# Block sums of the second layer's weights in a fused attention, Fourier-mix and MLP kernel: made once and kept in device memory, where they were made anew on GpSimd for each product

## The chip, the cores and the metric

The kernel runs on one core of a Trainium2 chip. The metric is the device time of one execution in microseconds (us), taken as the median of several runs. Everything is in 32-bit floats.

## The reference, cut to what matters

Four sequences of 768 rows pass through linear attention with eight heads of 64, then through a two-dimensional Fourier mix, a normalization and a two-layer network with a residual. The last part is the one that this case is about:

```python
x = attention(q, k, v, lam)                      # (4, 768, 512)
u = x + real(fft(fft(x, axis=1), axis=2))
un = (u - mean(u)) / sqrt(var(u) + 1e-6)
ch = maximum(un @ w_ch1, 0.0) @ w_ch2            # (512 x 2048), (2048 x 512)
out = u + ch
```

## The kernel before, in words

The 3072 rows of the network are handled in twelve groups of 256 rows. The first four groups (`PLAIN`) go through `mlp` (L629), ordinary matmuls that are woven between the attention and the Fourier mix. The other eight (`LATE`) wait in device memory: `utd` holds their normalized rows transposed, `ud` the rows for the residual. They are computed at the end, two groups (512 rows) at a time, by four calls of `late(j)` (L723), and these four calls fill the second half of the run.

`late` saves matmuls by the Strassen-Winograd scheme: a product of matrices cut into 2 x 2 blocks takes seven block products, not eight, at the price of sums of blocks before and after. The first layer uses one level of it, the second layer two.

- **The weights' first sums.** `combine_weights` (L680) makes the sums of blocks of `w1` and `w2` on VectorE (`w1s`, `w2s`, and two blocks in place). Part 0 runs beside the last plain groups, part 1 just before the first `late`. At the end of part 1 (L702 to L705) GpSimd replaces one quarter of each of the seven blocks of `w2` by a difference, `T3 = B22 - B12`.
- **Level one, L788 to L810.** Eight steps `i`, each of seven block products of two matmuls (`prod`, L765). ScalarE copies partial results out of PSUM (L780, L792, L799, L802), VectorE adds and applies the rectifier (L782 to L785, L794, L795, L803, L804). The hidden values lie in five tiles `h` ("ha", "hs" in the profile). In step `i` the matmul pair of `finish` (L776) for the step before reuses the PSUM bank that L803 must have read.
- **Level two, L865 to L919.** The seven products of the second layer (`PRODUCTS`, L721) are each cut once more, so each is seven steps of four matmuls (L875), 49 steps in a call. `level2` (L865) runs a product; two consecutive products are interleaved, step by step. Each step reads either a quarter of `h` or a sum of quarters (`S1, S2, S4`, tiles "sx", made on VectorE by `prepare_a`, L742), and either a quarter of the weights or a sum of quarters (`T1, T2, T4`, tiles "tx", made on GpSimd by `prepare_b`, L757). After each step `give` (L878) takes a PSUM bank into the output tiles `T` and `yt`, by VectorE (L883) or ScalarE (L881). `after(k)` (L838) makes the sums between products: `part_sum` (L829) splits two of them into a half on VectorE and a half on GpSimd (L831, L832), `add_u` (L825) adds the residual on GpSimd.
- **Buffers.** "tx" has six buffers, the sums of two products; "sx" has seven; PSUM has eight banks. "u2" (the residual rows) has two, `ur` (the transposed rows of a call) one.
- **Queues.** SyncE issues nearly all transfers, in order: the residual rows (L820), the next call's `ur` (L719) and the direct output stores (L623). Rows that belong in reversed order are stored by an indirect transfer that GpSimd issues (L625).

The order of the instructions on each engine is settled when the kernel is built, by a scheduler that follows the program order and the readiness of tiles; `tc.keep_in_program_order` pins an instruction. Each engine then works its list in order and stops at the first instruction whose inputs or buffers aren't ready.

Of the kernel before, what the change touches and what calls it, by code (L numbers as in the profile page):

```python
# [10 lines left out]
F32 = mybir.dt.float32  # L11
# [65 lines left out]
def kernel(  # L77
# [10 lines left out]
    nc = tc.nc  # L88
    B, H, S, D = q.shape
    DM = H * D  # L90
# [8 lines left out]
    HM = DM // 2  # L99
# [3 lines left out]
    G = 2  # L103
    NG = NC // G
    TT = [(t, HC + t) for t in range(HC)]
# [25 lines left out]
    dram = ctx.enter_context(tc.tile_pool(name="dram", bufs=1, space=bass.MemoryType.DRAM))  # L131
# [7 lines left out]
    def new(pool, shape, tag, **kw):  # L139
        cnt[0] += 1  # L140
        return pool.tile(shape, F32, tag=tag, name=f"{tag}{cnt[0]}", **kw)
# [268 lines left out]
    uts, utd, ud = {}, {}, {}  # L410
# [208 lines left out]
    PLAIN, LATE = ORDER[:4], ORDER[4:]  # L619
# [51 lines left out]
    ADD, SUB = ALU.add, ALU.subtract  # L671
    HF, FH = FO // 2, DFF // 2
    V = nc.vector
# [2 lines left out]
        pass  # L676

    s2 = Sum2()

    def combine_weights(part):  # L680

        k1, k2, f1, f2 = slice(0, 2), slice(2, 4), slice(0, FH), slice(FH, DFF)
        a11, a12, a21, a22 = w1[:, k1, f1], w1[:, k2, f1], w1[:, k1, f2], w1[:, k2, f2]
        b11, b12 = w2[:, 0:HF, 0:HM], w2[:, 0:HF, HM:DM]
        b21, b22 = w2[:, HF:FO, 0:HM], w2[:, HF:FO, HM:DM]
        if part == 0:
            ws = s2.ws = s2.wp.tile([128, 3, 2, FH], F32, name="w1s")
            wz = s2.wz = s2.wp.tile([128, 3, HF, HM], F32, name="w2s")
            todo = [(ws[:, 0], a21, a22, ADD), (ws[:, 1], ws[:, 0], a11, SUB), (ws[:, 2], a12, ws[:, 1], SUB),
                    (wz[:, 0], b12, b11, SUB), (wz[:, 1], b22, wz[:, 0], SUB), (wz[:, 2], b21, wz[:, 1], SUB)]  # L690
        else:

            ws, wz = s2.ws, s2.wz
            todo = [(a21, a11, a21, SUB), (b12, b22, b12, SUB)]
            s2.A = dict(a11=a11, a12=a12, a22=a22, s1=ws[:, 0], s2=ws[:, 1], s4=ws[:, 2], s3=a21)
            s2.B = dict(b11=b11, b21=b21, b22=b22, t1=wz[:, 0], t2=wz[:, 1], t4=wz[:, 2], t3=b12)
        for o, x, y, op in todo:
            n = o.shape[1]
            for i in range(0, n, n // 2):
                V.tensor_tensor(o[:, i:i + n // 2], x[:, i:i + n // 2], y[:, i:i + n // 2], op=op)  # L700
                yield 1.3
        if part:  # L702
            for b in s2.B.values():
                q = quarters_b(b)
                nc.gpsimd.tensor_tensor(q[1], q[3], q[1], op=SUB)  # L705

    def quarters_a(t):

        return [t[:, s, i:i + HF // 2] for s in range(2) for i in (0, HF // 2)]

    def quarters_b(t):

        return [t[:, i:i + HF // 2, m:m + HM // 2] for i in (0, HF // 2) for m in (0, HM // 2)]

    def load_u(j, queue=nc.sync):

        r = s2.u[j] = new(s2.up, [128, 2, KO, G * 128], "ur")
        for h, (b, g) in enumerate(LATE[2 * j:2 * j + 2]):
            queue.dma_start(r[:, h], utd[b, g])  # L719

    PRODUCTS = [("a11", "b11"), ("a12", "b21"), ("s3", "t3"), ("s2", "t2"), ("s4", "b22"), ("s1", "t1"), ("a22", "t4")]  # L721

    def late(j):  # L723
        r = s2.u.pop(j)
        b11, b21, b12, b22 = r[:, 0, 0:2], r[:, 0, 2:4], r[:, 1, 0:2], r[:, 1, 2:4]
        t1, t2, t4 = (new(s2.hp, [128, 2, G * 128], "sx", bufs=7) for _ in range(3))
# [6 lines left out]
        h = {n: new(s2.hp, [128, G, HF, 128], f"h{n}") for n in ("a11", "a12", "a22", "s1", "s3")}  # L733

        pre_a, pre_b = {}, {}

        def split(t):

            A11, _, A21, _ = quarters_a(t)
            V.tensor_tensor(A21, A11, A21, op=SUB)  # L740

        def prepare_a(k):  # L742

            a = PRODUCTS[k][0]
            A11, A12, A3, A22 = quarters_a(h[a])
            S1, S2, S4 = pre_a[k] = [new(s2.hp, [128, HF // 2, 128], "sx", bufs=7) for _ in range(3)]
            if a in ("a11", "a12", "a22", "s3"):
                split(h[a])
                yield 0.0
            V.tensor_tensor(S2, A22, A3, op=SUB)  # L750
            yield 0.0
            V.tensor_tensor(S1, S2, A11, op=ADD)  # L752
            yield 0.0
            V.tensor_tensor(S4, A12, S2, op=SUB)  # L754
            yield 0.0

        def prepare_b(k):  # L757

            B11, T3, B21, B22 = quarters_b(s2.B[PRODUCTS[k][1]])
            T1, T2, T4 = pre_b[k] = [new(s2.yp, [128, HF // 2, HM // 2], "tx", bufs=6) for _ in range(3)]  # L760
            for o, x, y, op in ((T2, T3, B11, ADD), (T1, B22, T2, SUB), (T4, B21, T2, SUB)):
                nc.gpsimd.tensor_tensor(o, x, y, op=op)  # L762
                yield 0.0

        def prod(ps, a, b, i, first):  # L765
            for kt in range(2):
                nc.tensor.matmul(ps, lhsT=s2.A[a][:, kt, 128 * i:128 * i + 128], rhs=U[b][:, kt, :],  # L767
                                 start=(first and kt == 0), stop=(kt == 1), skip_group_check=True)

        def two(t):  # L770
            return t.rearrange("p (s k) -> p s k", s=G)

        def bank():
            return new(s2.ps, [128, DM], "p2")[:, 0:G * 128]

        def finish(i, X, Z):  # L776
# [7 lines left out]
            V.tensor_tensor(s1, a21, a22, op=ADD)  # L784
            V.tensor_tensor(s3, a11, a21, op=SUB)  # L785

        last = None
        for i in range(HF):  # L788
            a11, a12, a22 = (h[n][:, :, i, :] for n in ("a11", "a12", "a22"))
            X, Y, Z = bank(), bank(), bank()  # L790
            prod(X, "a11", "b11", i, True)
            nc.scalar.copy(a11, two(X))  # L792
            prod(Y, "a12", "b21", i, True)
            V.tensor_tensor(a11, two(Y), a11, op=ADD)  # L794
            V.tensor_scalar(a11, a11, 0.0, None, op0=ALU.max)  # L795
            if last:
                finish(*last)
            prod(X, "s2", "t2", i, False)
            nc.scalar.copy(a12, two(X))  # L799
            prod(Z, "s3", "t3", i, True)  # L800
            prod(X, "s1", "t1", i, False)
            nc.scalar.copy(a22, two(X))  # L802
            V.tensor_tensor(a22, two(Z), a22, op=ADD)  # L803
            V.tensor_scalar(a22, a22, 0.0, None, op0=ALU.max)  # L804
            last = (i, X, Z)
            if i == HF // 2:
                for k in range(2):
                    run(prepare_b(k))
        run(prepare_a(0))
        finish(*last)  # L810
        run(prepare_a(1))
        if 2 * j + 2 < len(LATE):
            load_u(j + 1)

        who = [[(b, TT[g][s]) for s in range(G)] for b, g in LATE[2 * j:2 * j + 2]]
        us = []
        for k in who:
            us.append(new(s2.yp, [128, G, DM], "u2", bufs=2))
            for s in range(G):
                nc.sync.dma_start(us[-1][:, s], ud[k[s]])  # L820
        yt = new(s2.yp, [128, 2, G, DM], "y2")
        T = new(s2.yp, [128, G, HM], "t2")
        y11, y12, y21, y22 = (yt[:, k, :, m:m + HM] for k in range(2) for m in (0, HM))
# [1 line left out]
        def add_u(k, m, y):  # L825
            u = us[k][:, :, 0:HM] if m == 0 else us[k][:, :, DM - 1:HM - 1:-1]
            nc.gpsimd.tensor_tensor(y, y, u, op=ADD)

        def part_sum(o, x, y, op):  # L829

            V.tensor_tensor(o[:, 0], x[:, 0], y[:, 0], op=op)  # L831
            nc.gpsimd.tensor_tensor(o[:, 1], x[:, 1], y[:, 1], op=op)  # L832

        def stores(k, cols=slice(0, DM)):
            for s in reversed(range(G)):
# [2 lines left out]
        def after(k):  # L838

            if k == 0:  # L840
                split(h["s1"])
                h["s2"] = h["a11"]
                part_sum(h["a11"], h["s1"], h["a11"], SUB)
            elif k == 1:
                V.tensor_tensor(y11, y11, T, op=ADD)
                h["s4"] = h["a12"]
                part_sum(h["a12"], h["a12"], h["s2"], SUB)
                add_u(0, 0, y11)
            elif k == 3:
                V.tensor_tensor(y21, T, y22, op=ADD)  # L850
                add_u(1, 0, y21)
                add_u(1, 1, y22)
            elif k == 4:
                add_u(0, 1, y12)
            elif k == 5:
                V.tensor_tensor(y12, y12, T, op=ADD)
                stores(0)
                V.tensor_tensor(y22, y22, T, op=ADD)
                store(*who[1][0], yt[:, 1, 0], slice(HM, DM))
            elif k == 6:  # L860
                stores(1, slice(0, HM))
# [3 lines left out]
        def level2(k):  # L865

            (a, b), (y, fresh) = PRODUCTS[k], outs[k]
            A11, A12, A3, A22 = quarters_a(h[a])
# [38 lines left out]

        n = len(PRODUCTS)
        live = {}
        for at in range(7 * n + 8):  # L910
            k = at // 7
# [39 lines left out]
    def run(gen):  # L951
        return sum(gen)
# [51 lines left out]
    for j in range(len(LATE) // 2):  # L1004
        late(j)
# [30 lines left out]
```

## Time and profile before

| what | value |
|---|---|
| median of 3 runs (lowest to highest) | 849.95 us (847.34 to 852.95) |
| the profiled execution | 846.62 us |
| its span | 844.8 us |
| TensorE (PE) busy | 787.0 us, 93% |
| VectorE (DVE) busy | 581.3 us, 69% |
| ScalarE (ACT) busy | 203.1 us, 24% |
| GpSimd (POOL) busy | 282.2 us, 33% |
| mean granted TensorE clock | 0.991 |

A matmul of 32-bit floats is recorded as two TensorE instructions, so counts of matmuls in the profile are twice those of the program. The first call of `late` begins at about 429 us of the span, the others at 541, 640 and 738 us; the last matmul ends at 834 us. In the views below, a line of the timeline gives start, duration, engine, program line, operation, tiles and, in brackets, how long the engine had been idle and who released it.

### The profile page before, as it was taken

To read this page: it belongs to the slowest core of one execution; us is meant where nothing else is said; L and a number is where in the kernel's file an instruction comes from. 1 tells how busy PE (TensorE), PEld (TensorE's weight loads), DVE (VectorE), ACT (ScalarE), POOL (GpSimd) and SP (SyncE) were. 2 spreads that over 40 slices of the span, in tenths; PEclk is the share of its full clock that TensorE was granted. 3 is DMA by queue.
4 is the path that set the end of the run, shared out by engine and by line. 5 is a ranking of instruction groups with operands and counts; after the bars stand their busy time and mean duration, and the time that the engine had idled before them with its cause. 6 is when DMAs were issued, how large, how long until landed. Compare 5 with 4: busy or idle time off the path is not lost.

```text
span 844.8 us, 13570 instructions
## 1 busy us (share of the span) xinstructions
PE 787.0 (93%) x5280; PEld 645.1 (76%) x5280; DVE 581.3 (69%) x1158; ACT 203.1 (24%) x512; POOL 282.2 (33%) x217
## 2 busy tenths in 40 slices
PE   7989899999999999999978998999899998999995
PEld 5777767676676767778447898888898888988885
DVE  6899798857735832466974588756995578846982
ACT  3755434235321112211002210122101221022100
POOL 3223240111111101210180059800894029910593
PEclk9999999999999999999989999999999999999998
DMA  9969524369441255432230010200102010110001
GB/s 252 251 133 255 158 87 125 76 162 221 109 115 50 69 121 108 136 100 50 62 99 13 1 51 1 90 11 10 42 26 76 0 51 2 51 50 1 1 1 51
DMA packets 126694, 69.01 MB, mean 82 GB/s; under 512 B 111150, under 2 KB 112174, under 8 KB 126630
## 3 DMA queue, kind: packets, MB, share of 16 engines
q1 hardware_dynamic: 121488, 55.67, 26.0%
q0 software_dynamic: 2112, 6.69, 2.5%
q10 hardware_dynamic: 3030, 5.78, 1.9%
q8 instruction: 42, 0.69, 0.3%
q14 instruction: 22, 0.18, 0.1%
HBM read 48.72 MB, written 19.40 MB: 81 GB/s over the span
## 4 chain that ended last, share of the span: by engine, by line
PE 32%; POOL 8%; DVE 7%; issue 3%; DMA 1%; POOLq 0%; DVEq 0%; ACT 0%; ACTq 0%; SPq 0%
PE p L767 22%; PE p L875 9%; POOL tx L762 5%; POOL ha L832 3%; DVE w2s L700 1%; DVE w L700 1%; DMA out_dram<-y,ix 1%; DVE w1s L700 1%; DVE ur L730 1%; DVE y L850 1%; DVE t L883 1%; POOL w L705 1%; DVE sx L754 0%; DVE sx L752 0%; DVE sx L728 0%
## 5 line engine op out<-in xcount | busy, mean ns | idle before, releaser
L636 PE MATMUL pm<-ut,w 128*128 128x256 f32 x512 | 119.2, 382 | 0.0
L650 PE MATMUL pm<-w,hr 128*128 128x512 f32 x256 | 115.8, 597 | 0.1
L636 PEld LDWEIGHTS pm<-ut,w 128*128 128x128 f32 x512 | 94.4, 190 | 15.3 <-issue 3.6
L767 PE MATMUL p<-ur,w 128*128 128x256 f32 x384 | 94.8, 383 | 0.9 <-DVE y L662 0.9
L762 POOL TENSOR_TENSOR tx<-w 128x512 f32<-128x512 f32 x16 | 24.7, 1546 | 182.3 <-PE p L875 182.3
L650 PEld LDWEIGHTS pm<-w,hr 128*128 128x128 f32 x256 | 46.6, 190 | 49.5 <-issue 48.0
L767 PEld LDWEIGHTS p<-ur,w 128*128 128x128 f32 x384 | 73.6, 193 | 11.9 <-PE p L767 1.3
L767 PE MATMUL p<-sx,w1s 128*128 128x256 f32 x256 | 67.6, 388 | 1.8 <-DVE sx L728 1.8
L875 PE MATMUL p<-tx,sx 128*128 128x128 f32 x448 | 59.5, 276 | 5.3 <-DVE t L883 5.3
L875 PEld LDWEIGHTS p<-tx,sx 128*128 128x128 f32 x448 | 54.5, 192 | 6.0 <-issue 6.0
L767 PEld LDWEIGHTS p<-sx,w1s 128*128 128x128 f32 x256 | 49.6, 194 | 9.1 <-issue 2.2
L270 POOL TENSOR_TENSOR kd<-k,decay 128x512 f32<-128x512 f32 x20 | 23.7, 1186 | 95.4 <-PE pa L315 53.1
L762 POOL TENSOR_TENSOR tx<-w,tx 128x512 f32<-128x512 f32 x32 | 51.1, 1619 | 4.7 <-PE p L875 4.5
L803 DVE TENSOR_TENSOR ha<-p,ha 128x256 f32<-128x256 f32 x32 | 13.5, 423 | 54.8 <-ACT ha L802 54.8
L550 POOL TENSOR_SCALAR ve<-mv 128x2 f32<-128x2 f32 x12 | 3.4, 287 | 123.3 <-DVE mv L547 123.3
L881 ACT COPY y<-p 128x128 f32<-128x128 f32 x48 | 12.7, 266 | 119.7 <-PE p L875 119.7
L767 PE MATMUL p<-ur,w1s 128*128 128x256 f32 x128 | 34.2, 390 | 5.6 <-ACT ha L802 5.6
L762 POOL TENSOR_TENSOR tx<-w2s,tx 128x512 f32<-128x512 f32 x24 | 39.1, 1649 | 0.6
L875 PE MATMUL p<-w,ha 128*128 128x128 f32 x288 | 37.4, 275 | 0.0
L302 DVE TENSOR_TENSOR sc<-pa,decay 128x512 f32<-128x512 f32 x48 | 31.4, 682 | 8.3 <-PE pa L298 8.2
L298 PEld LDWEIGHTS pa<-qT,kT 64*128 64x128 f32 x384 | 26.0, 193 | 13.2 <-ACT qT L281 7.2
L875 PEld LDWEIGHTS p<-w,ha 128*128 128x128 f32 x288 | 35.3, 192 | 0.4
(172 smaller groups left out, 1587.7 us busy)
## 6 DMA issues: line engine op xcount, KB each, us to landing
raw<-in_moe_w_ch_dram SPq DMA_DIRECT2D x32, 512.0 KB, 5.0
k<-in_k_dram SPq DMA_DIRECT2D x24, 256.0 KB, 4.9
q<-in_q_dram SPq DMA_DIRECT2D x24, 256.0 KB, 5.8
v<-in_v_dram SPq DMA_DIRECT2D x24, 256.0 KB, 4.3
ud<-x SPq DMA_DIRECT2D x16, 256.0 KB, 2.3
utd<-e SPq DMA_DIRECT2D x64, 64.0 KB, 2.2
u<-ud SPq DMA_DIRECT2D x16, 256.0 KB, 2.9
ur<-utd SPq DMA_DIRECT2D x6, 512.0 KB, 4.2
```

The source lines that it names most:

```text
L270: nc.gpsimd.tensor_tensor(kd, kt, kpow, op=ALU.mult)
L298: mm(pss[hi][:, hp, :], lhsT=kT[HD[hi], hp, :], rhs=qT[HD[hi], hp, :], start=True, stop=True)
L302: nc.vector.tensor_tensor(t, pss[hi], decay[:, hi::2, :], op=ALU.mult)
L636: nc.tensor.matmul(ps, lhsT=w1[:, c, 128 * fc:128 * fc + 128], rhs=ut[:, c, :], start=(c == 0), stop=(c == KO - 1))
L650: nc.tensor.matmul(ps, lhsT=hr[(fc - f0) // 4][:, fc % 4, 128 * i:128 * i + 128], rhs=w2[:, fc, :], start=(fc == f0), stop=(fc == f1 - 1))
L700: V.tensor_tensor(o[:, i:i + n // 2], x[:, i:i + n // 2], y[:, i:i + n // 2], op=op)
L762: nc.gpsimd.tensor_tensor(o, x, y, op=op)
L767: nc.tensor.matmul(ps, lhsT=s2.A[a][:, kt, 128 * i:128 * i + 128], rhs=U[b][:, kt, :], start=(first and kt == 0), stop=(kt == 1), skip_gro ...
L803: V.tensor_tensor(a22, two(Z), a22, op=ADD)
L832: nc.gpsimd.tensor_tensor(o[:, 1], x[:, 1], y[:, 1], op=op)
L875: nc.tensor.matmul(ps, lhsT=a[:, i, :], rhs=b[:, i, :], start=(first and i == 0), stop=(i == HF // 2 - 1), skip_group_check=True)
L881: nc.scalar.copy(o, ps)
```

## The change

The sums `T1, T2, T4` of the weights are the same in all four calls of `late`. The changed kernel makes them once. In the first call, after each of the steps 0 to 6 of level one, `keep_sums(k)` makes the difference `T3` and the three sums of product `k` on GpSimd, in an order that is pinned, and stores the sums in 21 tensors `td` in device memory. `prepare_b` no longer computes: in all four calls it loads the three sums of a product into "tx" by SyncE. The loop over `s2.B` in `combine_weights` goes, since `keep_sums` does its work. `part_sum` does both halves on VectorE. The loads of the residual rows move into level one, to step 5, and the first two `prepare_b` to step 6. The five `split` (VectorE, in place) move from `prepare_a` and `after` into steps 5 to 7 of level one.

```diff
         for o, x, y, op in todo:
             n = o.shape[1]
             for i in range(0, n, n // 2):
                 V.tensor_tensor(o[:, i:i + n // 2], x[:, i:i + n // 2], y[:, i:i + n // 2], op=op)
                 yield 1.3
-        if part:
-            for b in s2.B.values():
-                q = quarters_b(b)
-                nc.gpsimd.tensor_tensor(q[1], q[3], q[1], op=SUB)
...
+    s2.td = []
+
+    def keep_sums(k):
+
+        pin = tc.keep_in_program_order
+        B11, B12, B21, B22 = quarters_b(s2.B[PRODUCTS[k][1]])
+        pin(nc.gpsimd.tensor_tensor(B12, B22, B12, op=SUB))
+        T1, T2, T4 = t = [new(s2.yp, [128, HF // 2, HM // 2], "tx", bufs=6) for _ in range(3)]
+        s2.td.append([dram.tile([128, HF // 2, HM // 2], F32, name=f"td{k}{i}") for i in range(3)])
+        for i, o, x, y, op in ((1, T2, B12, B11, ADD), (0, T1, B22, T2, SUB), (2, T4, B21, T2, SUB)):
+            pin(nc.gpsimd.tensor_tensor(o, x, y, op=op))
+            nc.sync.dma_start(s2.td[k][i], o)
...
         def prepare_a(k):
...
-            if a in ("a11", "a12", "a22", "s3"):
-                split(h[a])
-                yield 0.0
...
         def prepare_b(k):
 
-            B11, T3, B21, B22 = quarters_b(s2.B[PRODUCTS[k][1]])
-            T1, T2, T4 = pre_b[k] = [new(s2.yp, [128, HF // 2, HM // 2], "tx", bufs=6) for _ in range(3)]
-            for o, x, y, op in ((T2, T3, B11, ADD), (T1, B22, T2, SUB), (T4, B21, T2, SUB)):
-                nc.gpsimd.tensor_tensor(o, x, y, op=op)
+            pre_b[k] = [new(s2.yp, [128, HF // 2, HM // 2], "tx", bufs=6) for _ in range(3)]
+            for i in (1, 0, 2):
+                nc.sync.dma_start(pre_b[k][i], s2.td[k][i])
                 yield 0.0
...
+        def load_x():
+            for k in range(2):
+                for s in range(G):
+                    tc.keep_in_program_order(nc.sync.dma_start(us[k][:, s], ud[who[k][s]]))
...
             last = (i, X, Z)
-            if i == HF // 2:
+            if j == 0 and i < len(PRODUCTS):
+                keep_sums(i)
+            if i == HF - 3:
+                load_x()
+            if i == HF - 2:
                 for k in range(2):
                     run(prepare_b(k))
+            if i > HF // 2:
+                for n in (("a11", "s3"), ("a12", "s1"), ("a22",))[i - HF // 2 - 1]:
+                    split(h[n])
...
         def part_sum(o, x, y, op):
 
-            V.tensor_tensor(o[:, 0], x[:, 0], y[:, 0], op=op)
-            nc.gpsimd.tensor_tensor(o[:, 1], x[:, 1], y[:, 1], op=op)
+            for s in range(G):
+                V.tensor_tensor(o[:, s], x[:, s], y[:, s], op=op)
...
             if k == 0:
-                split(h["s1"])
                 h["s2"] = h["a11"]
```

More of the change, by code (lines that the diff above doesn't have):

```diff
@@ L678 @@
     s2 = Sum2()
+    PRODUCTS = [("a11", "b11"), ("a12", "b21"), ("s3", "t3"), ("s2", "t2"), ("s4", "b22"), ("s1", "t1"), ("a22", "t4")]
     def combine_weights(part):
@@ L719, in load_u @@
             queue.dma_start(r[:, h], utd[b, g])
-    PRODUCTS = [("a11", "b11"), ("a12", "b21"), ("s3", "t3"), ("s2", "t2"), ("s4", "b22"), ("s1", "t1"), ("a22", "t4")]
     def late(j):
@@ L785, in finish @@
             V.tensor_tensor(s3, a11, a21, op=SUB)
+        who = [[(b, TT[g][s]) for s in range(G)] for b, g in LATE[2 * j:2 * j + 2]]
+        us = [new(s2.yp, [128, G, DM], "u2", bufs=2) for _ in range(2)]
+        def load_x():
+            for k in range(2):
+                for s in range(G):
+                    tc.keep_in_program_order(nc.sync.dma_start(us[k][:, s], ud[who[k][s]]))
         last = None
@@ L813, in late @@
             load_u(j + 1)
[L815 to L820, printed above, removed]
         yt = new(s2.yp, [128, 2, G, DM], "y2")
```

## The prediction

> **What bounds the kernel now.** I read the page first, then the busy time by stage, then TensorE's waits in the second half, then the timeline where they occur.
>
> ```profile
> PE 787.0 (93%) x5280; PEld 645.1 (76%) x5280; DVE 581.3 (69%) x1158; ACT 203.1 (24%) x512; POOL 282.2 (33%) x217
> ```
>
> TensorE is the bound, 58 us short of the span. The diff touches nothing before 420 us, so I cut the rest into stages. Columns: stage, its length, PE busy, PEld, DVE, ACT, POOL, granted clock, DMA share, GB/s.
>
> ```profile
> 429.40:447.30 17.90, 9.58 (x30) 6.96 (x28) 9.29 (x10) 1.21 (x4) 13.93 (x10) 0.80 0.13 49
> 447.30:489.40 42.10, 42.10 (x188) 36.87 (x189) 24.10 (x64) 9.93 (x27) 0.00 (x0) 0.96 0.00 1
> 489.40:541.20 51.80, 47.03 (x402) 45.85 (x402) 44.68 (x66) 5.01 (x18) 43.74 (x26) 1.00 0.13 42
> 541.20:587.95 46.75, 46.75 (x220) 41.19 (x219) 26.15 (x67) 11.24 (x30) 4.46 (x4) 1.00 0.07 23
> ```
>
> Level one (fourth line) has no idle TensorE. Level two (third line) lacks 4.8 us, and there VectorE and GpSimd are both busy over 84%. The first level one (first two lines) has a bad start: 8.3 us idle, and a clock of 0.80. TensorE's waits from 489 to 835 us, the first line from 429 to 448 us:
>
> ```profile
> PE p L767 <- ACT ha L802: 5.6, 1, 5.6
> PE p L875 <- DVE t L883: 9.5, 11, 1.3
> PE p L875 <- DVE y L883: 8.5, 7, 1.8
> ```
>
> So level two waits 18.0 us for VectorE to take PSUM banks (L883). Why VectorE is late, the timeline shows; the last line is the same L754 with GpSimd idle.
>
> ```profile
> 800.91 3.26 POOL L762 TENSOR_TENSOR tx<-w2s,tx 128x512 f32<-128x512 f32 x2
> 801.48 1.56 DVE L752 TENSOR_TENSOR sx<-sx,ha 128x512 f32<-128x512 f32 x1
> 802.97 0.28 DVE L883 TENSOR_TENSOR y<-p,y 128x128 f32<-128x128 f32 x1
> 803.17 1.55 DVE L754 TENSOR_TENSOR sx<-ha,sx 128x512 f32<-128x512 f32 x1
> 803.30 1.16 PE L875 MATMUL p<-w,sx 128*128 128x128 f32 x8 [1.79 <-DVE y L883]
> ...
> 586.94 0.69 DVE L754 TENSOR_TENSOR sx<-ha,sx 128x512 f32<-128x512 f32 x1
> ```
>
> L752 and L754 take 0.69 us alone and 1.55 beside GpSimd; the L883 behind them is late, and TensorE stops for 1.79. GpSimd suffers alike: L762 takes 1.26 us alone and about 1.7 beside them. And the start:
>
> ```profile
> 441.12 2.48 POOL L762 TENSOR_TENSOR tx<-w,tx 128x512 f32<-128x512 f32 x2
> 443.77 1.08 POOL L625 DMA_INDIRECT out_dram<-y,ix  x1 [0.17 <-issue]
> 446.83 0.37 ACT L802 COPY ha<-p 128x256 f32<-128x256 f32 x1 [10.16 <-DMA out_dram<-y,ix]
> ```
>
> L802 writes a tile that lies where the last plain `y` lay, and the store that reads `y` is queued on GpSimd behind sums (L705, L762). TensorE stands 5.6 us for that.
>
> **What the Trainium skill says.** "SBUF — State Buffer", section "Who interferes with whom": VectorE instructions with two SBUF inputs, and `tensor_scalar` in its two-port mode, exclude a GpSimd instruction that reads SBUF; whichever comes second "fully blocks". The trace agrees: 0.69 against 1.55 us; the `tensor_scalar` L795 0.29 against 1.24; L883, with one PSUM input, keeps 0.28. The same section says that a DMA never contends with a compute engine; no view here contradicts it. "TensorE: Matmul & The Clock Gate", section "What's actually happening", says that after an idle window of about 3.4 us TensorE gets half its clock until it has been busy for as long. The trace has such stretches at 0.50 from 434 to 440 us, after the first waits, and from 447 to 450, after the 5.6 us.
>
> **The change part by part.**
>
> *Level two.* The 21 sums of `prepare_b` per call (those of two products run around the stage's edges) and two halves of `part_sum` (2.80 us each) leave GpSimd; only four L827 (1.3 us alone) stay. VectorE's excess over its durations alone, summed by form over the four calls (for instance L754 20 x (1.346 - 0.684) = 13.2, L831 4 x (3.169 - 1.21) = 7.8), is about 68 us, 17 per call; nearly all of it goes. VectorE gets two 128x1024 sums at 1.21 = 2.4 us per call. Its busy time falls from 44.7 to about 30 us in a stage of 46. Stepping through the built order from 493 us with these durations, every L883 is done 1 to 2 us before TensorE wants the bank. The `split`s do not move: in the order of both builds the five stand at the same place, beside step 5, where the trace shows no TensorE wait.
> The gain: a call takes 98.3 us from start to start (541.33 to 639.66). Undisturbed it takes 112 matmuls of 0.432 (level one) and 196 of 0.2233 (eight records in 0.893): 48.4 + 43.8 = 92.2. The loss is 6.1 in three calls, 4.3 in the last (96.5 to its last matmul), 22.6 in all. I leave 0.9 per call: **-19 us**. From both sides: 18 recorded waits less the remainder of a longer queue, 13, and all of 22.6.
>
> *Loads.* 21 loads of 256 KB per call, 5.5 MB. Same-sized `u<-ud` loads land in 2.9 us (longest 4.0), their issue takes SyncE 0.3 to 0.5. A "tx" buffer is freed by the step that read it two products before, 14 steps of 0.89 us = 12.5 earlier; taking off the read itself leaves 11. Three issues and a landing are 4.5 us: covered. Ahead of them on SyncE: `ur` (1 MB, issued at level one's end, landing 3.8 to 4.8 us; the third product's first load is needed about 12 us after that). The first two products' loads for the next call stand ahead of this call's output stores, so the stores go a few us later; nothing reads their buffer for 45 us. Cost 0; if the cover were gone, see the third rival.
>
> *Start.* In the built order the indirect store now stands ahead of all sums, so L802's wait goes: -5.6, and with it the half clock after it: 3.2 us at half speed = -1.6. Before that, L705 no longer stretches VectorE's L700 (1.55 to 1.80 against 1.1) and the t-sums L727, L728 (1.30 and 1.63 against 0.69): TensorE's first matmuls come about 1.7 earlier, and if that keeps its clock up another 3.2 (6.4 us at half). Together -8.9, up to -12.
>
> *GpSimd in the first level one.* 28 operations at 1.26 = 35 us alone. Level one has per step five VectorE instructions that exclude GpSimd (three `tensor_scalar`, two sums). If GpSimd always has work they alternate: a pair takes 1.26 + 0.13 to 0.27, so five take about 7.3 us, against TensorE's 6.05 per step. L803 stands in that VectorE list, and TensorE can bear about 1.8 us delay of it (its idle before L803 is 1.97). GpSimd starts at about 432, has some 20 operations left when the pipeline is full at 444, so four steps lose 1.25 each: 5. The splits of step 5 fall into its tail: five contending instructions more, about 1.3. Less what the slack absorbs: **+4.5**. Bounds: 0 (slack absorbs it) to +13 (8.5 us a step and the splits fully exposed). GpSimd is done at about 475; the stores and the first loads behind it need 5 us, the first sum is wanted at about 485: in time by 5.
>
> Sum: -19 - 8.9 + 4.5 = -23.4; half of the further clock gain, -1.6, makes **-25**. The profiled execution took 846.62 us (span 844.8), so 821.6; its runs' median is 3.3 above it: 849.95 - 25 = **825**.
>
> **The rivals.**
> 1. *VectorE becomes the bound in the first level one.* For: the alternation seen at 431 to 437 us (L727 to L730 take 1.75 each). Against: only 28 operations. Cost 13, start without the clock gain: 849.95 - 19 - 8.9 + 13 = 835.
> 2. *The waits for L883 stay*, because two whole `part_sum` now block VectorE for 1.2 us pieces. Against: 30 of 46 us busy. If half stays: 849.95 - 13 = 837.
> 3. *Loads gate level two*: slower than before. Five products in each of four calls refill "tx" late, 20 waits of L - 11 us for a landing L; they cost more than 25 us only if L exceeds 12.3. The page's slowest 256 KB loads are 5.8, beside 250 GB/s; here 125 are needed. At L = 13: 825 + 40 = 865.
> 4. *Start and clock gain in full, contention absorbed*: 849.95 - 21 - 12 = 817.
>
> **How the numbers follow.** Forecast 0.72, rivals 0.10, 0.07, 0.03, 0.08. The forecast's own range is 820 to 831. For eight in ten I reach to rivals 4 and 1: 817 to 836. This kernel's measurement tells about 1% (8.5 us) from no change. Within 1% would need cases 1 and 2 together (0.03, taken from theirs); slower is rival 3 (0.03); faster the rest, 0.94.
>
> **What would show it.** Right: TensorE's waits for L883's successor below 4 us in all; the L754-like sums at 0.69 us in level two; no wait for the indirect store; GpSimd busy from 432 to about 475; `tx` loads landing in 3 to 4 us with no TensorE wait on them. The first level one should show the `tensor_scalar` at over 1 us, and TensorE waiting there for VectorE some 5 us. Wrong: a TensorE wait for the `tx` loads, level two still near 51 us, or a half clock through the first level one.

## The result, and the profile after

The changed kernel takes 817.92 us (median of 4 runs, 817.4 to 821.88), the kernel before 848.64 beside it on the same chip: a ratio of 0.964, 95% interval 0.9592 to 0.9688. That is 31 us less, where the prediction had 25; 817.92 lies below the forecast's own range of 820 to 831 and at the lower edge of the wider one, 817 to 836. The profiled execution took 817.94 us, its span is 816.2; between the two profiled executions the difference is 28.7, since the one of before lay below its median and the one of after on it.

First the engines' line of the page after, which answers to the first line shown of before:

```profile
PE 778.7 (95%) x5280; PEld 640.5 (78%) x5280; DVE 549.1 (67%) x1166; ACT 203.4 (25%) x512; POOL 148.5 (18%) x146
```

TensorE has the same 5280 records and 8 us less busy time. Of these, 2.6 us lie in the first level one, where there is less half clock (four records last 2.07 us in it, as at 466.52 below, in place of 1.03), and 4.9 in the four level twos. The clock there is 1.00 in both kernels, but behind each stall of before the first eight records take up to 1.16 us, as at 803.30 in the prediction's lines, where eight undisturbed take 0.893. GpSimd has lost 134 us and VectorE 32, though VectorE was given eight more sums.

Then the busy time by stage, for the first call of `late`. Columns as before: stage, its length, PE, PEld, DVE, ACT, POOL, granted clock, DMA share, GB/s.

```profile
429.60:434.00 4.40, 3.23 (x13) 1.93 (x11) 4.16 (x6) 0.75 (x2) 3.04 (x3) 1.00 0.16 60
434.00:462.60 28.60, 28.58 (x132) 25.00 (x132) 28.01 (x37) 6.75 (x18) 27.82 (x21) 1.00 0.37 138
462.60:466.50 3.90, 0.18 (x1) 0.00 (x0) 3.90 (x5) 0.38 (x1) 3.82 (x3) 0.97 0.20 72
466.50:469.90 3.40, 3.38 (x9) 2.70 (x10) 3.37 (x4) 0.00 (x0) 3.32 (x3) 0.53 0.68 233
...
483.70:529.40 45.70, 45.70 (x402) 45.48 (x401) 33.18 (x68) 5.01 (x18) 7.09 (x5) 1.00 0.48 136
529.40:576.00 46.60, 46.60 (x219) 41.02 (x218) 25.20 (x67) 11.26 (x30) 0.97 (x1) 1.00 0.16 55
```

Level two (the fifth line shown) takes 45.70 us with TensorE busy in all of it, where it took 51.80 with 47.03 busy; VectorE's 44.68 there is 33.18. The first level one runs from 429.60 to 483.71, 54.1 us; before it ran from 429.36 to 489.44, 60.1 us. It has no bad start any more, but a hole at 462.60 and a half clock behind it (lines three and four). A level one with no hole takes 46.6 (last line).

All that TensorE waits for, in the second half, stands in three lines of the waits:

```profile
PE p L772 <- DVE ha L816: 3.7, 1, 3.7
PE p L772 <- DVE ur L739: 0.9, 1, 0.9
PE p L772 <- DVE sx L737: 0.2, 1, 0.2
```

The 18.0 us for the old L883 (now L896) are gone to the last tenth, and so is the 5.6 for the indirect store. The span fell by 28.6 us: 6.0 in the first level one and 22.8 in what follows it, while the first call begins 0.2 later. The 18.0 us of waits and the 4.9 us of longer matmuls behind them make the 22.8, to a tenth. After the first level one a call went from 98.33 to 92.18 us (529.43 to 621.61), which is the undisturbed 92.2 of the prediction's working.

Where the new hole comes from shows the timeline of VectorE and GpSimd around it. L749 is the five `split`, L816 the sum that takes the PSUM bank which the next matmuls need.

```profile
459.51 1.42 DVE L749 TENSOR_TENSOR ha<-ha 128x512 f32<-128x512 f32 x1
460.34 1.71 POOL L718 TENSOR_TENSOR w2s<-w2s 128x512 f32<-128x512 f32 x1
460.85 1.35 DVE L788 TENSOR_SCALAR ha<-ha 128x256 f32<-128x256 f32 x1
462.12 0.68 DVE L749 TENSOR_TENSOR hs<-hs 128x512 f32<-128x512 f32 x1
462.72 1.75 DVE L749 TENSOR_TENSOR ha<-ha 128x512 f32<-128x512 f32 x1
464.00 3.26 POOL L722 TENSOR_TENSOR tx<-w2s,tx 128x512 f32<-128x512 f32 x2
464.39 1.74 DVE L749 TENSOR_TENSOR hs<-hs 128x512 f32<-128x512 f32 x1
466.06 0.41 DVE L816 TENSOR_TENSOR ha<-p,ha 128x256 f32<-128x256 f32 x1
466.52 2.07 PE L772 MATMUL p<-sx,w 128*128 128x256 f32 x4 [3.74 <-DVE ha L816]
```

Four splits of 0.68 us each stand ahead of L816 in VectorE's list; three of them are stretched to 1.4 to 1.75 by GpSimd's sums (1.63 to 1.79 in place of 1.26), and TensorE stops for 3.74.

### The profile page after: what moved, and what is told of

Read it like the earlier page. It is cut to its first block, busy times and chain, and to the rows that moved or that the text cites. A ratio compares the mean times of both kernels' runs of the same rounds, so it can differ in the third digit from the quotient of the medians.

```text
span 816.2 us, 13700 instructions
## 1 busy us (share of the span) xinstructions
PE 778.7 (95%) x5280; PEld 640.5 (78%) x5280; DVE 549.1 (67%) x1166; ACT 203.4 (25%) x512; POOL 148.5 (18%) x146
## 4 chain that ended last, share of the span: by engine, by line
PE 76%; DVE 11%; DMA 5%; issue 4%; ACT 2%; POOL 1%; POOLq 0%; SPq 0%; ACTq 0%; DVEq 0%
PE p L772 21%; PE p L888 21%; PE pm L650 10%; PE pm L636 8%; PE pa L332 3%; PE pa L516 3%; PE pa L298 3%; DMA x<-xb,ix 2%; PE pa L328 2%; DMA raw<-in_moe_w_ch_dram 1%; PE pa L274 1%; PE pa L315 1%; PE pa L348 1%; PE pa L279 1%; DVE stt L546 1%
## 5 line engine op out<-in xcount | busy, mean ns | idle before, releaser
L650 PEld LDWEIGHTS pm<-w,hr 128*128 128x128 f32 x256 | 46.6, 190 | 49.4 <-issue 48.0
L841 POOL TENSOR_TENSOR y<-y,u 128x512 f32<-128x512 f32 x16 | 22.5, 1420 | 259.2 <-DVE y L858 203.8
L816 DVE TENSOR_TENSOR ha<-p,ha 128x256 f32<-128x256 f32 x32 | 13.5, 422 | 40.9 <-ACT ha L815 40.9
L772 PE MATMUL p<-sx,w 128*128 128x256 f32 x128 | 33.9, 388 | 3.7 <-DVE ha L816 3.7
L332 PE MATMUL pa<-sc,v 128*64 128x128 f32 x384 | 31.5, 281 | 4.0 <-DVE sc L302 3.9
L896 DVE TENSOR_TENSOR t<-p,t 128x128 f32<-128x128 f32 x68 | 19.6, 288 | 21.7 <-PE p L888 21.2
L298 PE MATMUL pa<-qT,kT 64*128 64x128 f32 x384 | 30.7, 292 | 3.2 <-ACT qT L281 2.9
```

Of the source, the lines that this page charges most:

```text
L298: mm(pss[hi][:, hp, :], lhsT=kT[HD[hi], hp, :], rhs=qT[HD[hi], hp, :], start=True, stop=True)
L332: mm(po[HD[hi], hp, :], lhsT=vt[:, 2 * hp + hi, :], rhs=sc[hi][:, hp, :], start=(c == 0 and hp == 0), stop=(hp == HP - 1), skip_group_chec ...
L650: nc.tensor.matmul(ps, lhsT=hr[(fc - f0) // 4][:, fc % 4, 128 * i:128 * i + 128], rhs=w2[:, fc, :], start=(fc == f0), stop=(fc == f1 - 1))
L896: V.tensor_tensor(o, ps, o, op=ADD)
```

## The experiments

Eleven kernels, in four groups, each group timed beside the kernel before on its chip. "Level one" is the first call's, from its first matmul to the first one of level two in the profiled execution; the next column is TensorE's recorded waits inside level two.

| kernel | median, us | ratio to before, 95% | level one, us | waits in level two, us |
|---|---|---|---|---|
| before | 847.4 to 849.6 | 1 | 60.1 | 18.0 |
| after | 817.92 | 0.9592 to 0.9688 | 54.1 | 0 |
| e1_sums_v | 850.99 | 1.0021 to 1.0083 | 61.4 | 15.0 |
| e2_half_pool | 818.72 | 0.9623 to 0.9688 | 55.4 | 0 |
| e3_pool_reads | 844.27 | 0.9938 to 0.9977 | 55.4 | 14.5 |
| e4_pool_writes | 818.40 | 0.963 to 0.9684 | 54.3 | 0 |
| e5_store_first | 846.6 | 0.9972 to 0.9994 | 58.9 | 18.1 |
| e6_late_splits | 812.58 | 0.9563 to 0.9613 | 48.6 | 0 |
| e7_three_tx | 819.67 | 0.9633 to 0.9684 | 54.2 | 0 |
| after_again | 818.93 | 0.9634 to 0.9685 | 54.2 | 0 |
| e8_diffs_on_v | 835.76 | 0.9791 to 0.986 | 47.4 | 18.0 |
| e9_gaps | 848.23 | 0.9975 to 1.0006 | 60.3 | 18.0 |
| e10_diffs_ahead | 825.41 | 0.9691 to 0.976 | 61.5 | 0 |
| e11_own_result | 837.2 | 0.9826 to 0.9884 | 48.6 | 18.1 |

### Which GpSimd work slows level two

**e1_sums_v** does to the kernel before only the smallest part of the change.

```diff
-            V.tensor_tensor(o[:, 0], x[:, 0], y[:, 0], op=op)
-            nc.gpsimd.tensor_tensor(o[:, 1], x[:, 1], y[:, 1], op=op)
+            for s in range(G):
+                V.tensor_tensor(o[:, s], x[:, s], y[:, s], op=op)
```

> The kernel before with one part of the change alone: part_sum does both halves on VectorE; the weights' sums stay on GpSimd. Theory (the 21 weights' sums beside VectorE's two-input sums are what makes VectorE late): GpSimd loses 11 of its 44 us of level two per call, so about a quarter of the level-two loss of 22.6 us goes, 4 us faster, at most 8, and TensorE still waits over 10 us for VectorE in level two. Rival (it was part_sum, with the wait of L750 for GpSimd's half, that held VectorE up): 15 us faster or more, TensorE's waits in level two below 5 us.

It is slower by 0.5%, so the small gain that I expected of it wasn't there either: the waits fell from 18.0 to 15.0 us, but the granted clock in its level twos is 0.96 to 0.97 in place of 1.00, and a call takes 99.08. The halves on GpSimd are not what level two waited for.

**e2_half_pool** is the reverse edit on the kernel after.

> The changed kernel with part_sum's second half back on GpSimd; the weights' sums stay in device memory. Theory: two GpSimd sums of 2.8 us per call meet VectorE, which has slack: 3 us slower than the changed kernel, at most 6. Rival (part_sum held VectorE up): 15 us slower than the changed kernel or more.

The same time as after, and no wait in level two: this part of the change neither costs nor gives.

**e3_pool_reads** puts GpSimd's 21 sums per call back beside the loads; their results are overwritten by the loads, so only their presence differs. **e4_pool_writes** puts three memsets in the place of each of those sums.

```diff
             for i in (1, 0, 2):
+                B11, _, B21, B22 = quarters_b(s2.B[PRODUCTS[k][1]])
+                nc.gpsimd.tensor_tensor(pre_b[k][i], B21, B22, op=SUB)
                 nc.sync.dma_start(pre_b[k][i], s2.td[k][i])
```

```diff
             for i in (1, 0, 2):
+                for _ in range(3):
+                    nc.gpsimd.memset(pre_b[k][i], 0.0)
                 nc.sync.dma_start(pre_b[k][i], s2.td[k][i])
```

> The changed kernel, and before each of the 21 loads of a call GpSimd also makes a sum of two blocks of weights into the buffer, which the load then overwrites (the sums serve nothing; the output stays the reference's). Nobody but the load waits for these sums, so only their use of SBUF beside VectorE returns. Theory (exclusion of two-input VectorE sums by reading GpSimd instructions): VectorE's sums go back to about 1.5 us, and 12 to 18 us of the gain are lost. Rival (the gain came from TensorE or VectorE no longer waiting for GpSimd's results): no more than 3 us slower than the changed kernel.

> As the run with the 21 extra sums, but with three memsets of the same buffer (about 0.5 us each by the page's memsets) in place of each sum: GpSimd is as busy and delays the loads as much, but reads nothing. Theory: two-input VectorE sums keep 0.69 us, no more than 3 us slower than the changed kernel. Rival (any GpSimd work, or loads that start 1.5 us later, costs): as slow as the run with the sums, 12 to 18 us slower than the changed kernel.

e3 gives 26 us of the gain back, more than expected; e4 gives nothing back. The groups of e4, from level two of the first call on, show how busy GpSimd is there (columns: busy us, mean ns, idle before):

```profile
L768 POOL MEMSET tx<- 128x512 f32 x234 | 117.8, 525 | 162.0 <-PE p L890 154.5
...
L758 DVE TENSOR_TENSOR sx<-sx,hs 128x512 f32<-128x512 f32 x8 | 5.5, 689 | 0.4
```

and the same rows in e3, where the sums are two groups:

```profile
L768 POOL TENSOR_TENSOR tx<-w 128x512 f32<-128x512 f32 x42 | 68.2, 1642 | 140.8 <-PE p L890 140.8
L768 POOL TENSOR_TENSOR tx<-w2s 128x512 f32<-128x512 f32 x36 | 58.1, 1628 | 10.5 <-PE p L890 10.5
...
L758 DVE TENSOR_TENSOR sx<-sx,hs 128x512 f32<-128x512 f32 x8 | 13.3, 1661 | 0.4
```

Beside 117.8 us of memsets VectorE's sums take 689 ns; beside 126.3 us of sums, which read, 1661. So it isn't GpSimd's being busy, nor the loads' coming later, but its reading: that is what "SBUF — State Buffer", section "Who interferes with whom", of the Trainium skill says of instructions that read. TensorE's waits in e3 are the old ones:

```profile
PE p L890 <- DVE y L898: 9.7, 7, 2.0
PE p L890 <- DVE t L898: 4.8, 7, 1.0
```

They sum to 14.5 in 14 stalls. TensorE's busy time in the four level twos is 8.9 us longer than in after: in part matmuls that last longer behind a stall, as in before, and in part a clock that falls behind some of the stalls (0.64 for 3.4 us behind the 2.04 us stall at 598.8). The first level one has 1.3 us more, as it has in e2, where GpSimd has no such sums. Together these are the 24.7 us between the two profiled executions.

### Whether the loads are covered

**e7_three_tx** leaves three buffers for the loaded sums, so that a load waits until the product just before has read the same buffer, not the one before that.

```diff
-            pre_b[k] = [new(s2.yp, [128, HF // 2, HM // 2], "tx", bufs=6) for _ in range(3)]
+            pre_b[k] = [new(s2.yp, [128, HF // 2, HM // 2], "tx", bufs=3) for _ in range(3)]
```

(with the same edit in `keep_sums`)

> The kernel after, with three buffers in place of six for the loaded sums, so that each load waits for the sums of the product before to be read. Theory (a load of 2.7 us is well covered by a product's 6.15 us): 0 to 3 us more than the kernel after, at most 821. Rival (the loads' cover is thin, and six buffers are what hides it): level two waits in most of its products, 20 us or more above the kernel after.

819.67 beside 818.93 for **after_again**, with overlapping intervals, and still no TensorE wait in level two. The loads land in 2.7 us (median; 2.5 to 3.2 in after from level two on, 2.5 to 4.5 in e7), so even half the buffers cover them.

> The kernel after, unchanged, on the same chip as the three others, for comparison: 817 to 819 us by every theory.

### What the first level one lost and gained

**e6_late_splits** moves the first call's five splits (five VectorE sums of 128x512; the expectation's "15" is my slip) to the end of step 6, where GpSimd has done its 28 sums.

```diff
-            if i > HF // 2:
+            if j == 0:
+                if i == HF - 2:
+                    for n in ("a11", "s3", "a12", "s1", "a22"):
+                        split(h[n], pin=True)
+            elif i > HF // 2:
```

> The kernel after, with the five splits of the first call (15 VectorE sums of which several are read beside GpSimd's block sums in step 4) moved to the end of step 6, when GpSimd has done its 28 instructions. Theory (what the start still loses is splits that run beside GpSimd and hold up L816): the TensorE wait of 3.7 us for L816 and the half clock after it (1.6 us) go, about 5 us less than the kernel after, 812 to 814 us. Rival (the steps themselves are at their bound, so the same loss turns up elsewhere, or the late splits make the end of level one wait): within 1.5 us of the kernel after, or slower.

812.58 us, 6.3 below the kernel after beside it. The timeline of e6 has the splits at 472.41 to 475.5, at 0.68 us each; level one takes 48.6 us in place of 54.1, at full clock. This is the fastest kernel of the study.

**e5_store_first** is the kernel before with the seven differences pinned behind the indirect store: it was to show that the start's gain is the place of the store.

```diff
-        if part:
-            for b in s2.B.values():
-                q = quarters_b(b)
-                nc.gpsimd.tensor_tensor(q[1], q[3], q[1], op=SUB)
...
+            if j == 0 and i < 4:
+                for n in PRODUCTS[2 * i:2 * i + 2]:
+                    q = quarters_b(s2.B[n[1]])
+                    tc.keep_in_program_order(nc.gpsimd.tensor_tensor(q[1], q[3], q[1], op=SUB))
```

> The kernel before, with one part changed: the seven T3 differences of the first call, which stand ahead of the indirect store on GpSimd, are made two at a time in steps 0 to 3 of that call, behind the store; the t sums stay where they are. Theory (the start's gain comes from the store no longer waiting behind those seven): the first level one shrinks from 60.1 us by 9 to 12, the waits of level two stay at 18 us, so about 837 to 840 us. Rival (the start's gain has another source, or the differences delay VectorE's work in the steps by as much): less than 3 us, 845 to 849.

By its time the rival won, and the trace says by which half: the wait for the store is gone, and another has come, for a VectorE sum that the differences keep back. The timeline of e5:

```profile
431.18 1.25 POOL L625 DMA_INDIRECT out_dram<-y,ix  x1 [25.37 <-DVE y L662]
432.13 10.68 DVE L726 TENSOR_TENSOR ur<-ur 128x512 f32<-128x512 f32 x1
432.46 3.70 POOL L805 TENSOR_TENSOR w<-w 128x512 f32<-128x512 f32 x3
436.12 1.25 POOL L805 TENSOR_TENSOR w2s<-w2s 128x512 f32<-128x512 f32 x1
437.34 1.25 POOL L805 TENSOR_TENSOR w<-w 128x512 f32<-128x512 f32 x1
438.56 2.47 POOL L805 TENSOR_TENSOR w2s<-w2s 128x512 f32<-128x512 f32 x2
441.00 1.25 POOL L758 TENSOR_TENSOR tx<-w 128x512 f32<-128x512 f32 x1
442.86 2.08 PE L763 MATMUL p<-ur,w 128*128 128x256 f32 x4 [9.40 <-DVE ur L726]
```

A VectorE sum of 0.68 us took 10.68, and ended half a microsecond after the eighth GpSimd sum in a row. Those seven had nothing to wait for (each 1.25 us, the time alone), so they came all together and not two per step. Three kernels, e8, e9 and e11, ask whether that is the whole story.

**e8_diffs_on_v** is e5 with the seven differences on VectorE (`V.tensor_tensor` for `nc.gpsimd.tensor_tensor`).

> The kernel before, with the seven T3 differences of the first call made by VectorE, two per step in steps 0 to 3, so that GpSimd has neither them nor anything else ahead of the indirect store and does only six sums in the first level one. Theory (the start of before is lost because the store stands behind the differences, and the store_first run lost its gain again only because seven GpSimd sums in a row locked out one VectorE sum for 10.7 us): the wait of 9.4 us in the store_first run is gone, the first level one takes 49 to 52 us, so 8 to 11 us below the kernel before (837 to 840). Rival (the start costs this much whatever stands ahead of the store): at most 3 us below the kernel before.

The first level one is 47.4 us, 12.7 less than before and shorter than I expected, at full clock, and the kernel 13.8 us faster by its median. The level-two waits are the old 18.0. This is the start's gain without the rest of the change.

**e10_diffs_ahead** undoes only that in the kernel after: the seven differences are again made at the end of `combine_weights`.

> The kernel after, with one part undone: the seven T3 differences are again queued on GpSimd as soon as the weights' sums are there, ahead of the indirect store, and the 21 sums follow in the steps as after has them. Theory (what the start gained is the place of the store): the wait for the indirect store comes back with the half clock that follows it, 5.6 + 3 us or somewhat more, so 8 to 11 us above the kernel after, 826 to 829. Rival (the start's gain came from elsewhere, such as the earlier sums of inputs on VectorE): within 2 us of the kernel after.

825.41 us; set against before it is 6 us above the after of the other chips (0.9725 against 0.9659), below the 8 to 11 expected. Its waits (first level one):

```profile
PE p L775 <- ACT ha L818: 9.0, 1, 9.0
PE p L775 <- DVE sx L740: 1.8, 1, 1.8
```

The wait behind the store is back, and longer than before's 5.6. One more sum stands ahead of the store, which is issued at 445.12, not 443.77, and TensorE is there 2.0 us sooner (its last matmul ahead of the wait ends at 439.65, in before at 441.67). It is sooner because the clock stays at 1.00 behind the same two waits, 0.94 and 1.79, that before has with a half clock after them: so with the store in the way that half clock costs nothing by itself, and it counts only when the store's wait is gone. Behind the store's wait e10 has 3.4 us at 0.50. The wait for L816 is absent: the first split begins at 471.06, when GpSimd has been done since 464.8. So the price is 7.4 us of level one net (61.5 against 54.1), a loss of about 13 with the 5.6 of the splits handed back.

The seven differences did two things at their old place: they kept the store back, and they stretched the VectorE sums that TensorE's first matmuls need (waits of 2.7 us in before and 3.2 in e10, 1.1 in after). e8 and e10 move both at once, and no kernel has the one without the other; by the waits, the store's part is the larger.

**e9_gaps** is e5 with a memset of 128x128 ahead of each difference; **e11_own_result** is e5 with a small GpSimd sum behind each, that reads what the difference wrote.

```diff
+                    tc.keep_in_program_order(nc.gpsimd.memset(new(s2.hp, [128, 128], "gap", bufs=1), 0.0))
                     tc.keep_in_program_order(nc.gpsimd.tensor_tensor(q[1], q[3], q[1], op=SUB))
```

```diff
                     tc.keep_in_program_order(nc.gpsimd.tensor_tensor(q[1], q[3], q[1], op=SUB))
+                    tc.keep_in_program_order(nc.gpsimd.tensor_tensor(new(s2.hp, [128, 1, 128], "gap", bufs=1), q[1][:, 0:1], q[1][:, 0:1], op=ADD))
```

> The store_first kernel, with a GpSimd memset of 128x128 ahead of each of the seven differences, which adds GpSimd work and changes nothing else. Theory (a VectorE sum gets in only when GpSimd's reading instructions leave a gap, and the seven differences leave none): VectorE's sum beside them takes about 2 us in place of 10.7, TensorE's wait for it falls from 9.4 to under 2, and the kernel comes out 6 to 10 us faster than the store_first run (837 to 840). Rival (the two engines' sums alternate one for one in any case, and the sum of 10.7 us waited for something else): as the store_first run, 846 to 848, or slower by the memsets.

My theory of the gap fell. In the timeline of e9 the same sum stays out for 11.69 us across seven memsets of 0.2 us:

```profile
434.90 11.69 DVE L726 TENSOR_TENSOR ur<-ur 128x512 f32<-128x512 f32 x1
435.20 0.22 POOL L805 MEMSET gap<- 128x128 f32 x1
435.38 1.28 POOL L806 TENSOR_TENSOR w<-w 128x512 f32<-128x512 f32 x1
436.58 0.22 POOL L805 MEMSET gap<- 128x128 f32 x1
...
444.78 1.25 POOL L758 TENSOR_TENSOR tx<-w 128x512 f32<-128x512 f32 x1
```

> The store_first kernel, with a GpSimd sum of 128x128 behind each of the seven differences that reads what the difference has just written, so that GpSimd has to wait for its own result after each (the six sums for the first products, which need the differences too, move up among them; one reading instruction more per difference, nothing else changes). Theory now (VectorE's waiting sum gets in where GpSimd waits for its own result; while ready GpSimd instructions follow one another it does not): VectorE's sum beside them takes 2 to 3 us in place of 10.7 to 11.7, TensorE's wait for it is 1 to 2 us, the first level one takes 48 to 51 us in place of 58.9, and the time is 836 to 841. Rival (VectorE's sum stays out until the whole series has ended, whatever GpSimd waits for): TensorE's wait for it is 9 us or more, 847 or above.

837.2 us, 9 less than e5 though GpSimd does more. The timeline of e11:

```profile
434.08 2.17 DVE L726 TENSOR_TENSOR ur<-ur 128x512 f32<-128x512 f32 x1
434.41 1.28 POOL L805 TENSOR_TENSOR w<-w 128x512 f32<-128x512 f32 x1
435.77 1.60 POOL L758 TENSOR_TENSOR tx<-w 128x512 f32<-128x512 f32 x1
436.18 1.75 DVE L725 TENSOR_TENSOR sx<-ur,sx 128x512 f32<-128x512 f32 x1
```

VectorE got in as soon as a GpSimd sum (L758) had to wait for the one before it (L805). The added sums (L806) begin only at 440.29, so here it was a sum of the first product, moved up, that had to wait. The row of seven is broken up as well, and this run doesn't tell that from the waiting. A difference, then a sum that reads it, is also the order in which the kernel after makes its sums; there the same VectorE sum (L739) took 2.17, too.

## Why the prediction was right, and where its terms were off

**Level two: right in kind, too small by 3.8 us.** Of a possible 22.6 the prediction left 0.9 per call for what might remain and took 19; nothing remains, and 22.8 came. The prediction didn't say what its loss of 22.6 holds beyond the 18.0 of recorded waits; the traces show 4.9 us of longer matmuls behind the 18 stalls, which went with them. The mechanism is shown from both sides: the sums taken out (no waits), put back (e3), replaced by writes (e4). VectorE's busy time in level two is 33.18, where the prediction had about 30. My own stepping through the built order had said that every L883 is done 1 to 2 us early; I discounted it without a reason. Of the 7.1 us between the forecast of 825 and 817.92, the other 3.3 come from the step from profile to median: I set the changed kernel's median as far above its profiled execution as before's was, and it lies on it.

**The first level one: the right sum from wrong terms.** Predicted: -8.9 and -1.6 for the start, +4.5 for GpSimd, net -6.0; measured -6.0. The start gave more: e6, which has the start and GpSimd's 28 sums but no collision of the splits, is 11.5 us below before in its first level one, with the clock at 1.00 from the first matmul on. That is nearly the whole of the "up to -12", of whose last 3.2, the clock, I took half: with the store out of the way the full clock counted. e8 (12.7) and e10 show that the cause is the seven differences ahead of the store. That the net is met to a tenth is luck: the start gave 1.0 more than predicted, and GpSimd's sums cost 1.1 more.

**Contention in the steps: wrong place.** I had five VectorE instructions per step alternating with GpSimd, 7.3 us a step, four steps losing 1.25, and the splits adding 1.3. In the trace of after the steps of VectorE (from L816 to L816) take 5.66, 6.65 and 5.65 us:

```profile
436.84 0.41 DVE L816 TENSOR_TENSOR ha<-p,ha 128x256 f32<-128x256 f32 x1
...
442.50 0.42 DVE L816 TENSOR_TENSOR ha<-p,ha 128x256 f32<-128x256 f32 x1
...
449.15 0.41 DVE L816 TENSOR_TENSOR ha<-p,ha 128x256 f32<-128x256 f32 x1
...
450.87 0.98 DVE L808 TENSOR_SCALAR ha<-ha 128x256 f32<-128x256 f32 x1
451.77 0.41 DVE L789 TENSOR_TENSOR hs<-a,ha 128x256 f32<-128x256 f32 x1
452.11 1.49 DVE L790 TENSOR_TENSOR hs<-ha,a 128x256 f32<-128x256 f32 x1
...
454.80 0.41 DVE L816 TENSOR_TENSOR ha<-p,ha 128x256 f32<-128x256 f32 x1
```

In the third step L808 waits for GpSimd, but L789 right behind it is in at once (0.41, its time alone), so four instructions wait, not five; in the second L789 waits too (1.43), and that step takes 6.65. The mean is 6.0, just under TensorE's 6.05, and TensorE waits in none of them: the steps lose nothing, but by a narrow margin (with the splits, VectorE is busy for 46.62 of the 48.55 us of e6's level one). The whole cost is the splits': 3.74 of waiting and 1.6 of half clock in the trace, and 5.6 by the level one of e6. The term of the sum that failed is the one I gave 1.3; the one I gave 5 was 0, and "+4.5" stood near the truth by accident. I had put the splits in GpSimd's tail without stepping its list to them. The gain of the start itself brought them forward, from 469.5 in before to 459.5, and there GpSimd had eight sums left. That TensorE would "wait there for VectorE some 5 us" was right (3.7 and the slow matmuls), and that the two engines meet there is shown by e6.

**Loads: right.** Cost 0 on a cover of 11 us against 4.5; a landing takes 2.7 us where I had 3 to 4. e7 shows that the cover holds with half the buffers, which puts the third rival far off. GpSimd was done at 473.3 us where I had about 475.

**The rivals.** The first (VectorE as the bound, 835) is ruled out, though narrowly: 6.0 us a step against 6.05, and no wait of TensorE in the steps. The second (waits kept by the two `part_sum`) by e1 and e2. The fourth (817) is the nearest in time, but not in kind: the start came in full, but the contention was absorbed in the steps only, not where the splits meet GpSimd. The time reached it because level two gave 3.8 more and the step to the median 3.3. With that gone too, as in e6, it is 812.6.

## What to carry to other kernels

Before you price a stretched instruction, ask what the other engine does while it runs: beside GpSimd instructions that only write, VectorE's sums kept their time; beside GpSimd's sums those of one form took 2.4 times as long on average, so moving those sums into transfers gave time back to VectorE, which was the one that mattered. When you move work of the one engine, step the other's list to the same moment; five sums moved by some 10 us were worth 6 us here. And look at what stands ahead of a store that frees a buffer: seven sums ahead of one indirect store, and beside the VectorE sums that TensorE needs first, cost 11 to 13 us, and an experiment that moved them let in a new stall of 9.4 us that hid this until its trace was read.

## What the runs showed of the hardware that I had not expected

- A VectorE sum with two SBUF inputs can be kept out for far longer than one GpSimd instruction: 10.7 us by eight ready sums in a row, 11.7 with memsets of 0.2 us between. It got in where GpSimd had to wait for its own result (2.17 us in e11 and in after). What exactly lets it in stays open: in the trace of before three L705 in a row, none of them reading the other's result, let VectorE in between (4.61 us for three in place of 3.76, and 1.30 and 1.63 for VectorE's two sums beside them). "SBUF — State Buffer", section "Who interferes with whom", says that whichever comes second fully blocks. Here the sum that was kept out has the earlier start in the profile (432.13 against 432.46 for the first GpSimd sum in e5, 434.90 against 435.38 in e9), and eight GpSimd sums went ahead of it.
- A VectorE instruction right behind one that has waited can get in at once: L789 behind L808 (0.41 behind 0.98), and a split behind L788 (0.68 behind 1.35). It does not always: L790 behind L789 takes 1.49.
- The clock fell to half behind a stall of 3.74 us (0.53 for 3.4 us). Of two equal stalls of 2.0 us in e3, the one that ends at 503.8 left it at 1.00, the one that ends at 600.8 cost it (0.64 for 3.4 us); and behind the same two waits (0.9 and 1.8 us) at the start of level one, before has 0.52 for 6.4 us, where e10 stays at 1.00. "TensorE: Matmul & The Clock Gate", section "What's actually happening", gives the window as about 3.4 us and says that it runs freely and does not restart with the kernel. The length of the slow stretches (3.4 us, or some two of it) and the unequal fate of equal stalls agree with that; how idle a window must be, no run here shows. The prediction took the half clock from 434 to 440 us for what a window of 3.4 us of idle brings, but the waits ahead of it are 2.7 us in all: that stalls well under the window can cost the clock I had not drawn from the page.
